# A fused local-attention and state-space kernel: the order of every engine written out by hand

## The chip, the cores and the metric

One core of one Trainium2 chip runs the kernel. It has five engines that run at once, each through its own queue in order: TensorE (PE, matrix products, with weight loads shown apart as PEld), VectorE (DVE), ScalarE (ACT), GpSimd (POOL) and SyncE (SP, which here only starts transfers). The metric is device time in microseconds (us) of one execution; the median of 3 runs counts.

## The reference: what is computed

Two independent layers read inputs of 2048 tokens by 448 channels in bfloat16, and their outputs stand side by side in one output of 2048 by 896.

Layer A is local attention with 16 heads of 28 channels. Each token looks at 8 keys: itself and the tokens 2, 4, ..., 14 before it.

```
qkv = x @ wqkv                         # 448 -> 3*448
idx = pos[:, None] - arange(8) * 2     # negative ones are masked out
logits = einsum("bhsd,bhswd->bhsw", q, k[idx]) * 28 ** -0.5
o = einsum("bhsw,bhswd->bhsd", softmax(logits), v[idx])
a = o @ wo
```

Layer B is a state-space recurrence with 448 complex states, run over all tokens:

```
h_t = exp(dt * Lambda) * h_(t-1) + B_bar x_t
y_t = 2 * Re(C h_t) + Dskip * x_t
```

## The kernel before

**Layer A.** Tokens lie as 128 partitions by 16 tokens (index j): partition p holds tokens 16p to 16p + 15. The input is transposed on PE into xTA (`g_xta`, four groups of four tokens, two PSUM banks a group, copied out by DVE at L249), and `proj(t, j)` makes queries (t = 0), keys (1) or values (2) of all tokens j with four products of 112 x 448 (L254), copied out by ACT (L258). A token's window reaches 14 back, so keys and values carry a halo of 14 rows from the partition before: three transfers from SBUF to SBUF each (L265, L271), while partition 0, which has nothing before it, is cleared by POOL (L140, L141). `logits(hf)` works on half the tokens at a time (hf = 1: j from 8 to 15): in four steps of two window positions, DVE multiplies queries and keys (L409, 7168 wide, into the buffer `pr`, which is u1), halves the channels by adding (L410, L412), and after every second step sums the rest (L414 to L417). `softmax(hf)` is DVE with one exponential on ACT (L429). Then `av` runs four groups of four tokens: for each of 8 window positions DVE multiplies attention and values (L460, seven buffers in turn, laid over the keys), and PE adds and transposes the result into four accumulators with 16 products against the identity (L465). ACT copies them out (L469), `wo_group` multiplies by wo (L477) and the rows are stored.

**Layer B.** Parameters are transposed, and DVE and ACT make the powers of the transition (sine, cosine, exponential), the block matrices R (L202, one block of 896 columns for each power), G for the input weights, and a table of angles (`tab`, L277 to L279, with 1792 columns of float32 worked out in u1 by DVE and then by three passes on ACT). Tokens are in chunks of 8; `ssm_in(hf)` runs through the 8 positions j of all 256 chunks for half of the states (4 tiles, then 3): four products a tile (L324), one with R for the step before (L329), copied to Z by ACT (L331). `ssm_scan(hf)` runs the recurrence over chunks: DVE multiplies by the table (L336, L337), PE recombines (L342, L343), DVE scans (L345), and the same back (L347 to L355). `ssm_mix(hf, j)` adds the carried state to each position (L362, L364) and `ssm_out(j, cb)` makes an output row block of 128 by 448 (L373, L375), copied by ACT and stored.

**What sets the order.** The program text lists stage after stage, but a planner with a cost model reorders it: each engine's queue is what the planner chose. In the trace the logits of layer A on DVE run between steps of layer B. All eight PSUM banks are one pool (`bank()`), handed out in turn; a product that needs a bank waits until what lay in it has been copied out. Buffers are shared over time: u1 is the input of layer A, then the angle work, then the logits' products, then wo; u2 is the input and weights of layer B, then Z; the logits and the attention lie over xTA.

Of the kernel before, what the change touches and what calls it, by code (L numbers as in the profile page):

```python
# [10 lines left out]
ALU = mybir.AluOpType  # L11
# [25 lines left out]
def kernel(  # L37
# [16 lines left out]
    nc = tc.nc  # L54
    V = nc.vector
# [35 lines left out]
    G = l2.rearrange("p a b n -> p (a b n)")[:, 0:2 * NT * 128].rearrange("p (r t n) -> p r t n", r=2, t=NT)  # L91
# [10 lines left out]

    def half_rows(src):
        return src.rearrange("(t i) d -> i t d", i=HS)

    load_w(1)
    for jg in (3, 2, 1, 0):
        SP.dma_start(xnA[:, 4 * jg:4 * jg + 4, :], xA_r[:, 4 * jg:4 * jg + 4, :])
    load_w(0)
    prow = const.tile([3 * NT, 2, HS], BF16, tag="prow")  # L110
# [14 lines left out]
    make_identity(nc, ident[:])  # L125
    swp = const.tile([128, 2, 128], BF16, tag="swp")
# [7 lines left out]
    hpib = const.tile([128, 1], F32, tag="hpib")  # L134
    POOL.memset(hpib[:], 0.5 * PI * SHR)
    kk = const.tile([128, NP], F32, tag="kk")
    POOL.iota(kk[:], [[1, NP]], base=1, channel_multiplier=0, allow_small_or_imprecise_dtypes=True)
    iot = const.tile([128, NC], F32, tag="iot")
    POOL.iota(iot[:], [[1, NC]], base=0, channel_multiplier=0, allow_small_or_imprecise_dtypes=True)
    POOL.memset(k_s[0:1, :, 0:HALO, :], 0.0)  # L140
    POOL.memset(v_s[0:1, 0:HALO], 0.0)  # L141
# [9 lines left out]
    tp = bank(BF16)  # L151
    PE.transpose(tp[:, 0:3 * NT], prow.rearrange("p a i -> p (a i)"), ident[0:3 * NT, 0:3 * NT])
    prm = pt_("prm", (128, 3, NT))
    V.tensor_copy(prm.rearrange("p a b -> p (a b)"), tp[:, 0:3 * NT])
    tp = bank(BF16)
    PE.transpose(tp[0:KT, 0:4], drow[:], ident[0:4, 0:4])
    dsk = pt_("dsk", (KT, 4))
    V.tensor_copy(dsk[:], tp[0:KT, 0:4])
    lre, lim, ld = prm[:, 0], prm[:, 1], prm[:, 2]

# [4 lines left out]

    kkb = kk.unsqueeze(2).to_broadcast(PW)
    dt = pt_("dt")
    ACT.activation(dt[:], ld, ACTF.Exp)
    are = tt(pt_("are"), dt[:], lre, ALU.mult)
    th = tt(pt_("th"), dt[:], lim, ALU.mult)  # L170
    rk = pt_("rk", PW)
    tt(rk[:], by_k(are), kkb, ALU.mult)
    ACT.activation(rk[:], rk[:], ACTF.Exp)
    f1 = pt_("f1")
    V.tensor_scalar(f1[:], th[:], 1.0 / (2 * PI), None, ALU.mult)
    fT = pt_("fT")
    V.tensor_scalar(fT[:], th[:], float(T) / (2 * PI), None, ALU.mult)
# [8 lines left out]
    yk = pt_("yk", PW)  # L186
    tt(yk[:], by_k(f1), kkb, ALU.mult)
    tk = pt_("tk", PW)
    sn = pt_("sn", PW)
    cs = pt_("cs", PW)  # L190
    sincos(sn[:], cs[:], yk[:], tk[:])
    tt(cs[:], cs[:], rk[:], ALU.mult)
    tt(sn[:], sn[:], rk[:], ALU.mult)
    coef = const.tile([128, T - 1, NT, 2], BF16, tag="coef")
    V.tensor_copy(coef[0:HS, :, :, 0], cs[0:HS, 0:T - 1])
    V.tensor_copy(coef[0:HS, :, :, 1], sn[0:HS, 0:T - 1])
    V.tensor_scalar(coef[HS:128, :, :, 0], sn[HS:128, 0:T - 1], -1.0, None, ALU.mult)
    V.tensor_copy(coef[HS:128, :, :, 1], cs[HS:128, 0:T - 1])

# [5 lines left out]
    def build_R(k0, k1):  # L205
        blocks(R[:, k0:k1].rearrange("p k t n -> p (k t) n"), coef[:, k0:k1].rearrange("p k t a -> p (k t) a"), (k1 - k0) * NT)

    build_R(0, 1)
    a1, b1 = cs[:, 0], sn[:, 0]
    nr = pt_("nr")  # L210
    V.tensor_scalar(nr[:], a1, -1.0, None, ALU.add)
    t0 = pt_("t0")
    den = tt(pt_("den"), lre, lre, ALU.mult)
    tt(t0[:], lim, lim, ALU.mult)
    tt(den[:], den[:], t0[:], ALU.add)
    V.reciprocal(den[:], den[:])
    gre = tt(pt_("gre"), nr[:], lre, ALU.mult)
    tt(t0[:], b1, lim, ALU.mult)
    tt(gre[:], gre[:], t0[:], ALU.add)
    tt(gre[:], gre[:], den[:], ALU.mult)  # L220
    gim = tt(pt_("gim"), b1, lre, ALU.mult)
    tt(t0[:], nr[:], lim, ALU.mult)
    tt(gim[:], gim[:], t0[:], ALU.subtract)
    tt(gim[:], gim[:], den[:], ALU.mult)
    cg = pt_("cg", (128, NT, 2))
    V.tensor_copy(cg[0:HS, :, 0], gre[0:HS])
    V.tensor_copy(cg[0:HS, :, 1], gim[0:HS])
    V.tensor_scalar(cg[HS:128, :, 0], gim[HS:128], -1.0, None, ALU.mult)
    V.tensor_copy(cg[HS:128, :, 1], gre[HS:128])
    cgb = const.tile([128, 2, NT, 2], BF16, tag="cgb")  # L230
    V.tensor_copy(cgb[:, 0], cg[:])
    tt(cgb[:, 1], cg[:], cgb[:, 0], ALU.subtract)
    blocks(G.rearrange("p r t n -> p (r t) n"), cgb.rearrange("p r t a -> p (r t) a"), 2 * NT)
    pm2 = pt_("pm2", (128, 1))
    POOL.memset(pm2[0:HS], 2.0)
    POOL.memset(pm2[HS:128], -2.0)
    V.tensor_tensor(dgD[:], ident[0:KT, 0:KT].unsqueeze(1).to_broadcast((KT, 4, KT)),
                    dsk.unsqueeze(2).to_broadcast((KT, 4, KT)), ALU.mult)


    def g_xta(jg):
        for k2 in range(2):
            tp = bank(BF16)
            tpv = tp[0:KT].rearrange("p (k j n) -> p k j n", k=2, j=4)
            for kk_ in range(2):
                for jj in range(4):
                    kt = 2 * k2 + kk_
                    PE.transpose(tpv[:, kk_, jj, :], xnA[:, 4 * jg + jj, KT * kt:KT * (kt + 1)], ident[:])
            V.tensor_copy(xTA[:, 2 * k2:2 * k2 + 2, 4 * jg:4 * jg + 4, :], tpv)  # L249

# [8 lines left out]

    for jg in (3, 2, 1, 0):  # L260
        g_xta(jg)
        for j in range(4 * jg + 3, 4 * jg - 1, -1):
            proj(1, j)
    for lo, hi in ((1, 65), (65, 113), (113, 128)):
        SP.dma_start(k_s[lo:hi, :, 0:HALO, :], k_s[lo - 1:hi - 1, :, J:JK, :])  # L265
    for j in range(J - 1, -1, -1):
        proj(0, j)
    for j in range(J - 1, -1, -1):
        proj(2, j)
    for lo, hi in ((1, 65), (65, 113), (113, 128)):  # L270
        SP.dma_start(v_s[lo:hi, 0:HALO], v_s[lo - 1:hi - 1, J:JK])  # L271


    ftab = u1.bitcast(F32)
    yy = ftab[:, 0:NT * NC].rearrange("p (t c) -> p t c", t=NT)
    tm = ftab[:, NT * NC:2 * NT * NC].rearrange("p (t c) -> p t c", t=NT)
    V.tensor_tensor(yy, iot.unsqueeze(1).to_broadcast((128, NT, NC)),  # L277
                    fT.unsqueeze(2).to_broadcast((128, NT, NC)), ALU.mult)
    sincos(tab[:, 1], tab[:, 0], yy, tm)  # L279
    build_R(1, T - 1)  # L280


    for t in range(NT):
# [6 lines left out]
    for j in range(T):  # L290
        tp = bank(BF16)
        tpv = tp[0:KT].rearrange("p (k c n) -> p k c n", k=4, c=2)
        for kt in range(4):
            for c in range(2):
                PE.transpose(tpv[:, kt, c, :], xnB[:, c, j, KT * kt:KT * (kt + 1)], ident[:])
        V.tensor_copy(xT[:, :, j, :], tp[0:KT].rearrange("p (k n) -> p k n", k=4))  # L296
    for t2 in range(4):
# [8 lines left out]
        V.tensor_scalar(Cw[:, 2 * t2:2 * t2 + n, :], tp[:, 0:n * D].rearrange("p (t n) -> p t n", t=n), pm2[:], None, ALU.mult)  # L306

# [6 lines left out]


    def ssm_in(hf):
        for j in range(T):
            banks = []
            for pr_ in pairs(halves[hf]):
                ps = bank()  # L320
                banks.append(ps)
                for i, t in enumerate(pr_):
                    for kt in range(4):
                        PE.matmul(ps[:, i * NC:(i + 1) * NC], BT[:, kt, t, :], xT[:, kt, j, :],  # L324
                                  start=(kt == 0 and i == 0), stop=(kt == 3 and j == 0 and i == len(pr_) - 1))
            for ps, pr_ in zip(banks, pairs(halves[hf])):
                if j > 0:
                    for i, t in enumerate(pr_):
                        PE.matmul(ps[:, i * NC:(i + 1) * NC], R[:, 0, t, :], Z[:, t, j - 1, :], start=False, stop=(i == len(pr_) - 1))  # L329
                n = len(pr_)  # L330
                ACT.copy(Z[:, pr_[0]:pr_[0] + n, j, :], ps[:, 0:n * NC].rearrange("p (t c) -> p t c", t=n))  # L331

    def ssm_scan(hf):
# [3 lines left out]
        V.tensor_tensor(scr[:, 1, ts], z7, tab[:, 1, ts], ALU.mult)  # L337
        for pr_ in pairs(halves[hf]):
# [4 lines left out]
            PE.matmul(ps[:, 0:n * NC], swp[:, 1], scr[:, 1, sl], start=False, stop=True)  # L343
# [3 lines left out]
        V.tensor_tensor(scr[:, 0, ts], z7, tab[:, 0, ts], ALU.mult)  # L347
# [36 lines left out]
    for j in range(T - 1):  # L384
        ssm_mix(0, j)
# [136 lines left out]
```

## Time and profile before

| what | us |
|---|---|
| median of 3 runs (204.83 to 205.46) | 205.44 |
| the profiled execution | 205.64 |
| its span, first to last instruction | 203.9 |
| PE busy | 169.4 |
| DVE busy | 155.6 |
| ACT busy | 92.3 |
| POOL busy | 13.4 |
| L254, 192 projection products | 42.0 |
| L409, 8 products of queries and keys | 31.1 |
| L460, 32 products of attention and values | 32.9 |
| L465, 512 products against the identity | 29.1 |

Busy times of different engines lie beside each other; what counts is which of them the others wait for. "Clock" is the TensorE clock that the chip granted, as a share of the full one: 0.933 in the mean over the span. A group's mean duration covers the pipeline, so products back to back follow each other more closely than their durations say. A wait is put down to the release that came last.

### The profile page before, as it was taken

To read this page: it belongs to the slowest core of one execution; us is meant where nothing else is said; L and a number is where in the kernel's file an instruction comes from. 1 tells how busy PE (TensorE), PEld (TensorE's weight loads), DVE (VectorE), ACT (ScalarE), POOL (GpSimd) and SP (SyncE) were. 2 spreads that over 40 slices of the span, in tenths; PEclk is the share of its full clock that TensorE was granted. 3 is DMA by queue.
4 is the path that set the end of the run, shared out by engine and by line. 5 is a ranking of instruction groups with operands and counts; after the bars stand their busy time and mean duration, and the time that the engine had idled before them with its cause. 6 is when DMAs were issued, how large, how long until landed. Compare 5 with 4: busy or idle time off the path is not lost.

```text
span 203.9 us, 3696 instructions
## 1 busy us (share of the span) xinstructions
PE 169.4 (83%) x1551; PEld 118.8 (58%) x1552; DVE 155.6 (76%) x169; ACT 92.3 (45%) x178; POOL 13.4 (7%) x24
## 2 busy tenths in 40 slices
PE   0798299999999999502799609999999999999993
PEld 0544045555579888400388405656566899797951
DVE  6989949209958999999999999999700499795102
ACT  2073034998683254400259306945645230707081
POOL 8950000000000000000000100000000000000000
PEclk9999759999999999965599966999999999999999
DMA  6999500870049200000000000033222100202023
GB/s 194 350 220 376 132 3 18 186 112 3 0 84 197 35 3 0 0 0 0 3 0 0 0 0 3 0 85 110 66 68 68 48 3 0 72 24 71 27 68 113
DMA packets 13061, 13.98 MB, mean 69 GB/s; under 512 B 4469, under 2 KB 12149, under 8 KB 12917
## 3 DMA queue, kind: packets, MB, share of 16 engines
q1 hardware_dynamic: 12973, 13.74, 25.6%
q8 instruction: 12, 0.20, 0.4%
q14 instruction: 5, 0.04, 0.1%
q10 hardware_dynamic: 71, 0.01, 0.0%
HBM read 6.89 MB, written 3.67 MB: 52 GB/s over the span
## 4 chain that ended last, share of the span: by engine, by line
PE 60%; DVE 37%; issue 1%; POOL 0%; DVEq 0%; POOLq 0%
PE b L254 19%; PE b L465 14%; PE b L373 10%; DVE u L409 9%; PE b L477 6%; DVE u L410 5%; DVE R L202 3%; PE b L364 3%; PE b L362 3%; DVE l L412 3%; DVE swp L130 2%; DVE xT L296 2%; DVE u L345 2%; DVE u L249 2%; PE b L375 2%; PE b L287 2%
## 5 line engine op out<-in xcount | busy, mean ns | idle before, releaser
L254 PE MATMUL b<-wbuf,u 112*128 112x448 bf16 x192 | 42.0, 385 | 5.4 <-DVE u L249 5.4
L460 DVE TENSOR_TENSOR k_s<-u,v_s 128x1792 bf16<-128x1792 bf16 x32 | 32.9, 1088 | 16.0 <-PE b L465 16.0
L409 DVE TENSOR_TENSOR u<-q_s,k_s 128x7168 bf16<-128x7168 bf16 x8 | 31.1, 3891 | 8.8 <-ACT tab L184 8.7
L254 PEld LDWEIGHTS <-u 112*128 112x128 bf16 x192 | 19.6, 105 | 26.4 <-DVE u L249 6.9
L465 PEld LDWEIGHTS <-k_s 128*112 128x112 bf16 x512 | 29.0, 130 | 0.3
L465 PE MATMUL b<-ident,k_s 128*112 128x128 bf16 x512 | 29.1, 219 | 0.0
L324 PE MATMUL b<-xT,BT 112*128 112x256 bf16 x224 | 27.7, 278 | 0.0
L324 PEld LDWEIGHTS <-BT 112*128 112x128 bf16 x224 | 22.3, 100 | 3.7 <-issue 0.6
L331 ACT CAST u<-b 128x512 bf16<-128x512 f32 (+1 forms) x32 | 15.5, 534 | 18.7 <-PE b L329 12.1
L373 PE MATMUL b<-Cw,u 128*128 128x448 bf16 x112 | 23.8, 352 | 0.0
L469 ACT CAST q_s<-b 112x512 bf16<-112x512 f32 x16 | 8.2, 596 | 22.8 <-PE b L465 22.8
L410 DVE TENSOR_TENSOR u<-u 128x3584 bf16<-128x3584 bf16 x8 | 16.2, 2024 | 0.1
L373 PEld LDWEIGHTS <-u 128*128 128x128 bf16 x112 | 10.5, 97 | 7.5 <-ACT u L365 0.9
L258 ACT CAST k_s<-b 128x448 bf16<-128x448 f32 x16 | 8.3, 531 | 14.6 <-PE b L254 14.6
L377 ACT CAST yo<-b 128x448 bf16<-128x448 f32 x16 | 8.5, 531 | 13.1 <-PE b L375 8.2
L365 ACT CAST u<-b 128x512 bf16<-128x512 f32 (+1 forms) x28 | 13.2, 566 | 0.9 <-PE b L364 0.9
L477 PE MATMUL b<-u,q_s 112*128 112x448 bf16 x64 | 12.6, 352 | 0.0
L355 ACT CAST u<-b 128x512 bf16<-128x512 f32 (+1 forms) x4 | 2.0, 533 | 22.4 <-PE b L354 22.4
L412 DVE TENSOR_TENSOR l<-u 128x1792 bf16<-128x1792 bf16 x8 | 8.7, 1091 | 3.2 <-PE b L287 3.1
L362 PE MATMUL b<-u,ident 128*128 128x512 bf16 (+1 forms) x28 | 10.7, 381 | 0.0
L353 PE MATMUL b<-wbuf,ident 128*128 128x512 bf16 (+1 forms) x4 | 2.3, 566 | 9.7 <-DVE wbuf L347 9.7
L364 PE MATMUL b<-u,R 128*128 128x255 bf16 x49 | 10.3, 290 | 0.0
(123 smaller groups left out, 203.2 us busy)
## 6 DMA issues: line engine op xcount, KB each, us to landing
u<-in_A_x_dram SPq DMA_DIRECT2D x4, 448.0 KB, 4.7
u<-in_B_x_dram SPq DMA_DIRECT2D x2, 896.0 KB, 13.1
out_dram<-yo SPq DMA_DIRECT2D x16, 112.0 KB, 1.8
out_dram<-ya SPq DMA_DIRECT2D x16, 112.0 KB, 1.7
wbuf<-in_A_wqkv_dram SPq DMA_DIRECT2D x3, 392.0 KB, 5.1
k_s<-k_s SPq DMA_DIRECT2D x1, 784.0 KB, 6.7
v_s<-v_s SPq DMA_DIRECT2D x1, 784.0 KB, 5.9
k_s<-k_s SPq DMA_DIRECT2D x1, 588.0 KB
```

Of the source, the lines that this page charges most:

```text
L254: PE.matmul(ps[:, 0:D], xTA[:, kt, j, :], wts[:, t, kt, :], start=(kt == 0), stop=(kt == 3))
L324: PE.matmul(ps[:, i * NC:(i + 1) * NC], BT[:, kt, t, :], xT[:, kt, j, :], start=(kt == 0 and i == 0), stop=(kt == 3 and j == 0 and i == le ...
L331: ACT.copy(Z[:, pr_[0]:pr_[0] + n, j, :], ps[:, 0:n * NC].rearrange("p (t c) -> p t c", t=n))
L362: PE.matmul(ps[:, 0:n * NC], ident[:], Z[:, sl, j, :], start=True, stop=False)
L364: PE.matmul(ps[:, i * NC + 1:(i + 1) * NC], R[:, j, t, :], Z[:, t, T - 1, 0:NC - 1], start=False, stop=(i == n - 1))
L373: PE.matmul(ps[:, 0:D], Z[:, t, j, cols], Cw[:, t, :], start=(t == 0), stop=False)
L409: V.tensor_tensor(pr[:], qv, kv, ALU.mult)
L410: V.tensor_tensor(pr[:, :, 0:14, :], pr[:, :, 0:14, :], pr[:, :, 14:28, :], ALU.add)
L412: V.tensor_tensor(l2[:, sl], pr[:, :, 0:7, :], pr[:, :, 7:14, :], ALU.add)
L460: V.tensor_tensor(pv, attn[:, s, JG * H * jg:JG * H * (jg + 1)].rearrange("p (j h) -> p j h", h=H) .unsqueeze(2).to_broadcast((128, JG, DH ...
L465: PE.matmul(acc[kt][0:KT, jj * 128:(jj + 1) * 128], pvf[:, jj, KT * kt:KT * (kt + 1)], ident[:], start=(s == 0 and jj == 0), stop=(s == W ...
L477: PE.matmul(ps[:, 0:D], oT[:, kt, jj, :], wo_p[:, kt, :], start=(kt == 0), stop=(kt == 3))
```

## The change

The planner is switched off (`tc.manual_schedule()`), so that each engine runs its work in the order of the program text, and the text is rewritten to say that order. In parts:

- Loads: x group 3, key weights, x groups 2 and 1, query weights, x group 0 (before: key weights, x groups 3 to 0, query weights).
- 44 products of the identity with itself come first on PE; their result isn't used.
- The halo clears on POOL go; partition 0's halo rows are filled by one more transfer each for keys and values, from its own rows (finite numbers, masked later as before).
- Keys are projected for j from 15 to 6 first, then queries 15 to 8, keys 5 to 0, all values (with the input weights of layer B among them), and queries 7 to 0 last, with layer B's input transposes among them. Four of these eight transposes are copied out by ACT, the others by DVE.
- G lies in the last two blocks of R instead of a buffer of its own, and R is built block by block (seven times 896 columns) instead of one and six.
- DVE work that nothing waits for at once (parameters, R, tables, logits, softmax, value products) goes into a list. Two running sums, of PE work and of DVE work, are kept with costs in microseconds written into the program; after each PE step, list items are put into the program while the DVE sum is behind. `need` forces an item that the next step reads.
- The scans are cut into steps (`scan_mul`, `scan_pe`, `scan_run`, `scan_out`) placed among the input sums of the other half and the mixing; the C weights are transposed in between.
- Value products run up to 7 ahead of `av`; each `wo` step follows an odd window position of the next group instead of standing between groups. Two of the last four accumulator copies move to DVE.

The core of the diff:

```diff
+    ctx.enter_context(tc.manual_schedule())
-    G = l2.rearrange("p a b n -> p (a b n)")[:, 0:2 * NT * 128].rearrange("p (r t n) -> p r t n", r=2, t=NT)
+    G = R[:, T - 3:T - 1]
+    load_x(3)
     load_w(1)
-    for jg in (3, 2, 1, 0):
-        SP.dma_start(xnA[:, 4 * jg:4 * jg + 4, :], xA_r[:, 4 * jg:4 * jg + 4, :])
+    load_x(2)
+    load_x(1)
     load_w(0)
+    load_x(0)
...
+    warm = bank()
+    for _ in range(44):
+        PE.matmul(warm[:, 0:128], ident[:], ident[:], start=True, stop=True)
...
-    POOL.memset(k_s[0:1, :, 0:HALO, :], 0.0)
-    POOL.memset(v_s[0:1, 0:HALO], 0.0)
+    todo = []
+    load = [8.0, 8.0]
+    def pump(lead=0.0):
+        while todo and load[1] < load[0] + lead and (todo[0][2] is None or todo[0][2]()):
+            pop()
+    def need(*items):
+        while any(item in todo for item in items):
+            pop()
+    def pe(cost):
+        load[0] += cost
+        pump()
+    def dve(cost):
+        load[1] = max(load[1], load[0]) + cost
...
+    def halo(dst_of):
+        for lo, hi in ((1, 65), (65, 113), (113, 128)):
+            SP.dma_start(dst_of(lo, hi, 0, HALO), dst_of(lo - 1, hi - 1, J, JK))
+        SP.dma_start(dst_of(0, 1, 0, HALO), dst_of(0, 1, J, JK))
+    g_xta(3)
+    params_in()
+    add(1.6, params1)
+    add(1.2, params2)
+    add(2.5, params3)
+    has_G = add(2.0, build_G)
+    has_R = [add(1.0, lambda: build_R(0))]
+    for j in (15, 14, 13, 12):
+        proj(1, j)
+    g_xta(2)
+    for j in (11, 10, 9):
+        proj(1, j)
+    g_xta(1)
+    for j in (8, 7, 6):
+        proj(1, j)
+    g_xta(0)
+    has_tab = add(6.2, tables)
+    has_D = add(0.6, build_D)
+    for j in range(15, 7, -1):
+        proj(0, j)
+    logits(1, 0, 3)
+    for j in range(5, -1, -1):
+        proj(1, j)
+    halo(lambda lo, hi, a_, b_: k_s[lo:hi, :, a_:b_, :])
+    logits(1, 1, 2)
+    logits(1, 2, 1)
+    logits(1, 3, 0)
+    need(has_G)
+    for j in range(15, -1, -1):
+        proj(2, j)
+        if j % 2 == 0 and j < 14:
+            b_weights(j // 2)
+    for k in range(1, T - 1):
+        has_R.append(add(1.0, lambda k=k: build_R(k)))
+    halo(lambda lo, hi, a_, b_: v_s[lo:hi, a_:b_])
+    for j in range(7, -1, -1):
+        proj(0, j)
+        b_x(j)
+    for n_, g in enumerate((0, 1, 2, 3)):
+        logits(0, n_, g)
+    sm1, sm0 = softmax(1), softmax(0)
+    add(2.4, sm1[0])
+    add(2.4, sm0[0])
+    add(3.5, sm1[1])
+    add(3.5, sm0[1])
+    for j in range(T):
+        if j == 1:
+            need(has_R[0])
+        ssm_in(0, j)
+    need(has_tab)
+    scan_mul(0)
+    for t2 in range(4):
+        c_weights(t2)
+    ssm_in(1, 0)
+    banks = scan_pe(0, 1)
+    scan_run(banks)
+    scan_mul(0)
+    for j in range(1, 6):
+        ssm_in(1, j)
+    banks = scan_pe(0, 0)
+    scan_out(banks)
+    ssm_in(1, 6)
+    ssm_in(1, 7)
+    scan_mul(1)
+    for j in range(3):
+        need(has_R[j])
+        ssm_mix(0, j)
+    banks = scan_pe(1, 1)
+    scan_run(banks)
+    scan_mul(1)
+    need(has_D, *has_R)
+    for j in range(3, 7):
+        ssm_mix(0, j)
+    banks = scan_pe(1, 0)
+    scan_out(banks)
...
+    has_wo = add(0.0, wo_load)
+    for i in range(32):
+        add(1.09, lambda i=i: pv_mul(i), lambda: count[0] < count[1] + NPV)
+    ssm_mix(1, 0)
+    for cb in range(2):
+        ssm_out(T - 1, cb)
+    for j in range(T - 1):
+        if j + 1 < T - 1:
+            ssm_mix(1, j + 1)
+        for cb in range(2):
+            ssm_out(j, cb)
+    for i in range(32):
+        while count[0] <= i:
+            pop()
+        pump(7.0)
+        av(i)
+        n_, _, s = steps[i]
+        if n_ > 0 and s % 2 == 1:
+            wo_j(n_ - 1, s // 2)
+    for jj in range(JG):
+        wo_j(3, jj)
```

`logits` now adds its multiply (cost 3.9), its two halvings (2.0 and 1.1) and, after every second step, the rest of the sums (2.6) to the list as separate items.

## The prediction

> **What bounds the kernel now.** I read the page first, then the chain, the waits, busy time by stretch, and the timeline of the places the chain points to. From the page, busy time by engine and the 40 slices:
>
> ```profile
> PE 169.4 (83%) x1551; PEld 118.8 (58%) x1552; DVE 155.6 (76%) x169; ACT 92.3 (45%) x178; POOL 13.4 (7%) x24
> PE   0798299999999999502799609999999999999993
> DVE  6989949209958999999999999999700499795102
> PEclk9999759999999999965599966999999999999999
> PE 60%; DVE 37%; issue 1%; POOL 0%; DVEq 0%; POOLq 0%
> ```
>
> PE (the matrix engine) is busy 83%, yet the chain is 37% DVE (the vector engine). PE has holes at slices 4, 16 to 18 and 22 to 23, and behind each PEclk falls. DVE has its own holes at 38 to 46 us and after 148. So neither engine is full; the order leaves one waiting for the other. The stretches:
>
> ```profile
> 24.00:31.00 7.00, 6.94 (x32) 3.28 (x32) 4.19 (x14) 2.13 (x4) 0.00 (x0) 0.56 0.01 2
> 84.50:91.50 7.00, 0.00 (x0) 0.00 (x0) 6.93 (x6) 0.69 (x2) 0.00 (x0) 0.77 0.00 0
> 91.50:100.00 8.50, 3.36 (x7) 0.92 (x9) 8.50 (x13) 0.48 (x1) 0.32 (x3) 0.50 0.01 2
> 114.50:122.00 7.50, 1.06 (x5) 0.42 (x6) 7.50 (x13) 0.72 (x2) 0.62 (x4) 0.80 0.00 0
> ```
>
> (Columns: stretch, length, busy PE, PEld, DVE, ACT, POOL, clock, DMA.) At 84.5 to 100 and 114.5 to 122 PE waits for the two scans, queued on DVE behind logits. The waits and timeline name the rest:
>
> ```profile
> DVE u L409 <- ACT tab L184: 8.7, 1, 8.7
> DVE k_s L460 <- PE b L465: 16.0, 3, 12.8
> 1.93 5.35 POOL L140 MEMSET k_s<- 1x6272 bf16 x1
> 2.18 5.14 DVE L130 TENSOR_SCALAR swp<-swp 128x128 bf16<-128x128 bf16 x1
> 17.57 5.75 DVE L202 TENSOR_TENSOR R<-dup,coef 128x5376 bf16<-128x5376 bf16 x1
> 24.06 6.16 PE L254 MATMUL b<-wbuf,u 112*128 112x448 bf16 x16 [4.56 <-DVE u L249]
> 31.51 27.41 PE L254 MATMUL b<-wbuf,u 112*128 112x448 bf16 x144 [0.34 <-DVE u L249]
> ```
>
> The 5.75 us R block holds a transpose copy back, PE idles 4.56 us, and the next 16 projections take 0.385 us each instead of 27.41/144 = 0.190. From 122 us PE runs unbroken to 200.4 while DVE has run dry.
>
> **The change part by part.** I sum along the chain that I expect, against the profiled execution: 205.64 us, span 203.9, 1.74 around it; the median, 205.44, is 0.2 lower.
>
> *Halo clears.* Two POOL clears of 5.35 go. Three DVE rows beside them took 5.14, 2.79 and 2.73; like rows elsewhere take 0.27 and 0.17 (three times), so about 10 us of DVE go, partly off the chain. Instead each halo gets a fourth transfer. The key halo took 33.84 to about 45.2 (DMA busy 0.85 to 45, 0.08 after): 11.3. The fourth is unseen; a gain is excluded, the third's issue took 3.0, so 0 to 3; I take 1, as it moves one partition: 12.3. Keys end near 38.3, the halo lands at 50.7, and the first product that reads it starts at 52.9: hidden, with 2.2 to spare.
>
> *Start.* x group 3 goes ahead of the key weights on SP; x took 4.4 to 5.0 from issue, so it lands by 5.7. Meanwhile 44 identity matmuls run from 1.6; at the cold rates of before (0.375 x 128/448 = 0.107; cold transposes 1.96/16 = 0.122) they take 4.7 to 5.4. Transposes start near 6.9, as in before (6.76), but the clock may be up by then; cold projections cost before 5.27 - 3.04 = 2.2. At worst they delay PE 0.7.
>
> *DVE to the end of the tables.* The diff's two running sums of cost decide where a queued step lands in program order. Followed through, the tables land after query projection 12, the first logits after key projection 1, R1 to R6 among the last inputs of the first half, the first value product after output 14. First copies begin at 7.9. Two copies 1.3, parameter copies 0.4, chain to the sine 1.6: 11.2. ACT's table load (1.28) and sine hold DVE to 12.9; behind it wait the copies of group 2, so PE idles 1.9. Then 1.2 coefficients, 1.3 copies, 2.5 for cg, 0.2 wait, 1.3, G 2.0, 1.3, R0 1.1, angles 2.05 + 1.13 + 2.03: 12.9 + 16.1 = 29.0.
>
> *The new stall.* ACT's tables (1.70 + 1.74 + 1.87 = 5.3) stand in ACT's queue after query copy 12, waiting for DVE until 29.0; ten projections' copies queue behind. PE fills the 8 PSUM banks (8 x 0.76 = 6.1) and stops about 4.0, until 34.9. The first logits need both the shared buffer u1 and queries 8 to 15: 34.3 + four copies of 0.5 = 36.4, against 45.9 before.
>
> The row nearest to this stall is the 4.56 us idle before 24.06, after which the clock was 0.56 over 24 to 31. By it the next 3.4 to 6.8 us run at half speed, 1.7 to 3.4 lost on PE; DVE isn't held, as its inputs are computed. [...]
>
> *DVE from the first logits to the first value product.* One behind the other, each waiting for the last: 45.90 to 49.83, 51.89 and 53.02 are 3.93 + 2.06 + 1.12 = 7.1 a step, 8 steps 56.9; sums 0.97 + 0.70 + 0.70, four times, 9.5; softmax 2.76 + 3.73, twice, 13.0. Interleaved, before hid about 0.11 of each; written this way it is paid, some 5 us. R blocks 6 x 1.07 = 6.4; four xT copies 2.4; Cw 2.1; table products 4 x 0.60 + 4 x 0.47 = 4.3; scans 7 x 0.60 = 4.2. Together 98.8, with 1.5 waits for transposes 100.3. Start: 36.4 + 100.3 = 136.7.
>
> Four xT copies go to ACT; no row shows that form. Between 0.59 (512 wide) and 1.87 (1792 wide), nearest by width about 1.0, beside 2.4 of PE for each pair of token groups: covered up to about 1.9.
>
> *PE over the same time.* From 34.9, at the full-clock spacing of before: 26 projections by 0.76 19.8; BT 3.2 and transposes 3.8 (3.29 and 3.74 busy); 224 + 49 input products by 0.109 (16 in 1.74) 29.7; C 1.5; scan products 14 by 0.215 3.0; mix 10.6 (28 identity and 49 R products at 0.215 and 0.108, the short ones at half); sixteen outputs by 1.525 (chain: 1.32 + 0.20) 24.4: 96.0. Waits: 0.9 for the last xT, 1.2 and 1.1 for scans . With 1.6 for the clock: 135.7. So PE stands 2 us ahead of DVE, and its two large waits for scans are gone; what is late next is the first value product, at 137.7.
>
> *The end.* From there PE has 512 x 0.0558 = 28.6 and 64 x 0.19 = 12.1, nine waits of 0.11 for products (1.005 made against 0.894 used), two short bank waits 0.3 and 0.25 for the last copies, two of which move to DVE: 179.9. Before, wo's groups lay between accumulators and covered their copies; interleaved, one group at a time does. The last group's four copies on two engines (1.2) stand behind one projection (0.76). On SP the four wo loads stand behind the output stores: issued at about 137, four by 0.8 and 5 to land (the row of the x loads), 145, first needed at 148.
>
> From the last PE instruction to the end of the span was 203.9 - 200.4 = 3.5; 183.4, and 1.74 around: 185.1. I add 1 for a second clock drop at the 1.9 wait, between none and 2: **186.1**, in medians 185.9; I say 186.
>
> **The rivals.**
>
> A, PE is the bound: DVE's 0.11s overlap after all and the clock stays up. Then 134.1 + 41.7 + 5.2 = 181.0. For it: PE's 96.0 are rows at full clock. Against it: a 4 us hole.
>
> B, more waits than I see: the halo 2 late, both clock drops whole (7), the start 3 late by the parameter chain on ACT: 2 + 3 + 6 more of clock on 186 is 197 with all of it, 190 with some. For it: strict order makes ACT and DVE block on their heads (4.0 and 1.9 already).
>
> C, the written order isn't what runs, and only clears, load order and warm matmuls act: 205.6 minus 2.2 and the 4.56 + 3.1 at 24 us, about 196 to 203. The order before differs from program order, so an order is being made somewhere; little else speaks for it.
>
> D, slower: the clock stays at half after the 31 to 35 us stall, because waits keep recurring. Each microsecond at half speed costs 0.5; from 186 it takes 39 us of it to reach 205.4. At half speed to the end of the inputs, 34.9 to 85, PE's 46 us would cost 46 more: about 230. Against it: the longest slow stretch before was near 14 us (88 to 102), with 4 us holes inside; here PE is back to back after 35.
>
> **How the numbers follow.** The forecast (183 to 190) has 0.62, A (179 to 183) 0.12, B 0.16, C 0.03, D 0.06, no change 0.01; 0.3% is about what a measurement tells from none. Faster 0.93, same 0.01, slower 0.06. Range 181, A's bound, to 196, most of B: it leaves out part of A and B, C and D, under 2 in 10.
>
> **What would show it.** Right: first logits product near 36, after ACT's tables; PE idle once near 31 to 35 and not at 84 to 100; DVE unbroken from 64 to 168; first value product near 137; PE unbroken from 138. Wrong: logits starting after the halo (then 14 more); PE idle before scan products; half clock beyond 45 us; a store or wo load holding ACT or PE; value products ready well before PE, so that PE is the bound.

## The result and the profile after

The changed kernel takes 183.72 us (median of 4 runs, 183.64 to 184.47) against 205.45 of the kernel before beside it: a ratio of 0.895, 95% interval 0.892 to 0.899. The prediction was 186.0, in a range from 181 to 196. The profiled execution took 183.74, its span 182.0, so 1.74 around it as before; PE's clock was 0.979 in the mean.

The page of the changed kernel, busy time by engine and the 40 slices of 4.55 us each:

```profile
PE 167.4 (92%) x1596; PEld 123.2 (68%) x1596; DVE 150.3 (83%) x172; ACT 95.8 (53%) x180; POOL 2.8 (2%) x22
PE   6968996599999899999999899999959999999992
DVE  1358992399997899999999999999999999996031
PEclk9999999789999999999999999999996999999999
```

Counted from 0, PE has three visible holes left: slices 2 to 3 (where PE waits for the second pair of transpose copies), 6 to 7 and 29. The clock falls behind the last two. The holes at 84 to 100 and 114 to 122 us are gone; DVE runs without a break from slice 14 to slice 35. The sum closes: PE's idle time in the span went from 203.9 - 169.4 = 34.5 to 182.0 - 167.4 = 14.6, which is 19.9, and its busy time fell by 2.0; 21.9 together, and the profiled executions differ by 205.64 - 183.74 = 21.9. No PE work was saved: the 44 added products are inside the 167.4.

The changed kernel's timeline at the places that the prediction named (start, length, engine, line, operation, tiles, what it waited for):

```profile
7.13 1.29 DVE L296 COPY u<-b 112x1024 bf16<-112x1024 bf16 x2 [4.08 <-PE b L295]
12.10 0.22 DVE L187 TENSOR_TENSOR sn<-sn,rk 128x56 f32<-128x56 f32 x1 [1.50 <-ACT sn L198]
14.25 2.66 PE L303 MATMUL b<-wbuf,u 112*128 112x448 bf16 x12 [2.06 <-DVE u L296]
33.73 6.38 PE L303 MATMUL b<-wbuf,u 112*128 112x448 bf16 x24 [3.67 <-ACT q_s L307]
35.01 3.89 DVE L445 TENSOR_TENSOR u<-q_s,k_s 128x7168 bf16<-128x7168 bf16 x1 [6.50 <-ACT q_s L307]
135.83 10.85 PE L519 MATMUL b<-ident,k_s 128*112 128x128 bf16 x160 [2.26 <-DVE k_s L505]
```

The reader is to see three things: the sine holds DVE's queue to 12.10 and PE to 14.25; the angle table's three ACT passes hold the query copies, so PE stops for 3.67 and the first logits start at 35.01; and the first value product comes 2.26 after PE asks for it. Of PE's waits only two more are over 0.5 once the work has started (engine, tile, line, whom it waited for: total, times, longest):

```profile
PE b L360 <- DVE xT L327: 0.8, 1, 0.8
PE b L410 <- ACT u L401: 0.7, 1, 0.7
```

### The profile page after: what moved, and what is told of

The parts are those of the page before. It is cut to its first block, busy times and chain, and to the rows that moved or that the text cites. A ratio compares the mean times of both kernels' runs of the same rounds, so it can differ in the third digit from the quotient of the medians.

```text
span 182.0 us, 3801 instructions
## 1 busy us (share of the span) xinstructions
PE 167.4 (92%) x1596; PEld 123.2 (68%) x1596; DVE 150.3 (83%) x172; ACT 95.8 (53%) x180; POOL 2.8 (2%) x22
## 3 DMA queue, kind: packets, MB, share of 16 engines
HBM read 6.89 MB, written 3.67 MB: 58 GB/s over the span
## 4 chain that ended last, share of the span: by engine, by line
DVE 41%; PE 39%; DMA 10%; ACT 4%; issue 3%; SPq 1%; ACTq 0%; DVEq 0%
PE b L519 17%; PE b L303 12%; DVE u L445 11%; DMA u<-in_B_x_dram 7%; PE b L535 7%; DVE u L448 4%; DVE R L204 4%; DVE l L451 3%; DMA prow<-in_B_log_dt_dram 3%; DVE u L394 2%; PE b L325 2%; PE b L315 2%; DVE l L454 2%; DVE wbuf L375 1%; DVE wbuf L376 1%
## 5 line engine op out<-in xcount | busy, mean ns | idle before, releaser
L519 PEld LDWEIGHTS <-k_s 128*112 128x112 bf16 x512 | 32.0, 135 | 4.1 <-DVE k_s L505 2.4
L519 PE MATMUL b<-ident,k_s 128*112 128x128 bf16 x512 | 32.3, 225 | 2.3 <-DVE k_s L505 2.3
L303 PEld LDWEIGHTS <-u 112*128 112x128 bf16 x192 | 18.1, 100 | 22.4 <-issue 5.9
L360 PE MATMUL b<-xT,BT 112*128 112x256 bf16 x224 | 26.9, 272 | 0.8 <-DVE xT L327 0.8
L367 ACT CAST u<-b 128x512 bf16<-128x512 f32 (+1 forms) x32 | 15.6, 535 | 18.4 <-PE b L366 14.8
L540 ACT CAST ya<-b 128x448 bf16<-128x448 f32 x14 | 7.5, 538 | 18.0 <-PE b L535 13.3
L535 PE MATMUL b<-u,q_s 112*128 112x448 bf16 x64 | 14.1, 352 | 0.0
L528 ACT CAST q_s<-b 112x512 bf16<-112x512 f32 x14 | 7.2, 596 | 11.7 <-PE b L519 11.7
L411 ACT CAST u<-b 128x512 bf16<-128x512 f32 (+1 forms) x28 | 13.1, 558 | 0.2 <-PE b L410 0.2
L307 ACT CAST v_s<-b 128x448 bf16<-128x448 f32 x16 | 8.5, 532 | 3.3 <-PE b L303 3.3
L307 ACT CAST q_s<-b 128x448 bf16<-128x448 f32 x16 | 8.2, 535 | 3.5 <-PE b L303 3.5
```

The lines of the kernel that those rows point to most:

```text
L303: PE.matmul(ps[:, 0:D], xTA[:, kt, j, :], wts[:, t, kt, :], start=(kt == 0), stop=(kt == 3))
L307: ACT.copy(dst, src)
L411: ACT.copy(Z[:, sl, j, :], ps[:, 0:n * NC].rearrange("p (t c) -> p t c", t=n))
L519: PE.matmul(acc[kt][0:KT, jj * 128:(jj + 1) * 128], pvf[:, jj, KT * kt:KT * (kt + 1)], ident[:], start=(s == 0 and jj == 0), stop=(s == W ...
L535: PE.matmul(ps[:, 0:D], oTs[n_ % 3][:, kt, jj, :], wo_p[:, kt, :], start=(kt == 0), stop=(kt == 3))
```

## Experiments

All ratios are against the kernel before, run beside each on the same chip. The changed kernel was not run again beside them, so a difference from it in us compares medians of separate sets of runs (the kernel before had 205.25 to 205.49 in these sets); a few tenths of a microsecond of it are noise.

**1. Only the planner off.** Which part of the result is the switch, and which the text written for it? (This also tests rival C, that the written order isn't what runs.)

```diff
     nc = tc.nc
+    ctx.enter_context(tc.manual_schedule())
     V = nc.vector
```

> The kernel before with the planner switched off and nothing else: every engine runs in the order of the old text, all of layer B ahead of the logits. Theory (the new text's interleaving is the gain): DVE reaches the first logits only after the second scan, near 120 us, then needs about 80 us of logits and softmax with PE idle, then 43 us of value products and 5 of tail: 235 to 255 us. Rival (the planner's order was the loss in itself): 206 or less.

Measured, in two runs: 257.42 (256.35 to 258.48), ratio 1.254 (1.242 to 1.266). The written order is what runs, and the old text is a bad order: it is 52 us slower, some 2 us more than the upper end expected. PE's longest wait in that trace (engine, tile, line, whom it waited for: total, times, longest; "issue" means that the profile shows no cause):

```profile
PE b L466 <- issue: 49.0, 1, 49.0
```

In the text's order all logits stand behind all of layer B, and PE does nothing for 49.0 us before the first value product. So the switch by itself gains nothing; the gain comes with the rewritten text, 257.4 to 183.7 under the same switch. That text holds smaller edits beside the order. Two of them are taken back below (the clears, the identity products); the load order, G's new place, R in blocks and the copies moved between ACT and DVE were not tried by themselves.

**2. Only the halo clears, in the old kernel with its planner.** The prediction gave about 10 us of DVE time to the clears.

```diff
-    POOL.memset(k_s[0:1, :, 0:HALO, :], 0.0)
-    POOL.memset(v_s[0:1, 0:HALO], 0.0)
...
+    SP.dma_start(k_s[0:1, :, 0:HALO, :], k_s[0:1, :, J:JK, :])
...
+    SP.dma_start(v_s[0:1, 0:HALO], v_s[0:1, J:JK])
```

> The kernel before, planner on, only the two POOL clears replaced by one more transfer for each halo. Theory: the three DVE rows held beside the clears fall from 10.7 us together to about 0.6, but the 5.75 us R block and both scan holes stay: 201 to 205 us. Rival (the clears carry the gain): 190 to 196.

Measured: 205.40 (203.91 to 205.76), ratio 0.999 (0.996 to 1.002): nothing. DVE's busy time fell from 155.6 to 148.6, which is 7.0 and not the prediction's 10, since two of its three rows lie over each other (2.79 from 9.82 us and 2.73 from 9.90), and the span stayed at 203.9. Its timeline shows why:

```profile
12.96 0.22 DVE L146 TENSOR_TENSOR sn<-sn,rk 128x56 f32<-128x56 f32 x1 [2.20 <-ACT sn L180]
14.59 0.69 DVE L247 COPY u<-b 112x1024 bf16<-112x1024 bf16 x1 [0.72 <-PE b L246]
17.51 5.75 DVE L200 TENSOR_TENSOR R<-dup,coef 128x5376 bf16<-128x5376 bf16 x1
24.00 6.16 PE L252 MATMUL b<-wbuf,u 112*128 112x448 bf16 x16 [4.56 <-DVE u L247]
```

The time that the clears took came back as waits, for the sine (2.20) and for PE's next transposes (0.72); the R block that holds the copies starts at 17.51 instead of 17.57, and PE's 4.56 of idle is unchanged. In the old order the clears lay beside slack. My expectation counted them as gain by themselves and was wrong.

**3. The change with its clears back on POOL.** The same part, undone in the new order.

```diff
     POOL.memset(swp[:], 0.0)
+    POOL.memset(k_s[0:1, :, 0:HALO, :], 0.0)
+    POOL.memset(v_s[0:1, 0:HALO], 0.0)
...
-        SP.dma_start(dst_of(0, 1, 0, HALO), dst_of(0, 1, J, JK))
```

> The changed kernel with the two halo clears back on POOL and the two extra transfers gone. Theory: POOL is busy from 2.3 to about 13 us, the two scaling rows on DVE end with it (about 2.7 us each instead of 0.17), the chain to the tables and the first logits is 3 to 4 later: 186.5 to 188 us. Rival (hidden beside the load of x): within 0.5 of 183.7.

Measured: 190.97 (190.96 to 191.07), ratio 0.930 (0.925 to 0.936), 7.25 us slower than the changed kernel. The direction was expected, the size was not. The timeline of that kernel:

```profile
2.23 5.32 POOL L146 MEMSET k_s<- 1x6272 bf16 x1
7.49 5.35 POOL L147 MEMSET v_s<- 1x6272 bf16 x1
2.33 5.25 DVE L148 COPY swp<-ident 64x64 bf16<-64x64 bf16 x1 [2.33 <-POOL swp L145]
7.59 5.28 DVE L149 TENSOR_SCALAR swp<-ident 64x64 bf16<-64x64 bf16 x1
13.16 1.28 DVE L298 COPY u<-b 112x1024 bf16<-112x1024 bf16 x2
41.01 5.25 PE L305 MATMUL b<-wbuf,u 112*128 112x448 bf16 x18 [3.67 <-ACT q_s L309]
```

Two copies of 64 x 64, 0.17 and 0.18 in the changed kernel, each last until the clear beside them ends (7.58 against 7.55, 12.87 against 12.84). The first transpose copy starts at 13.16 instead of 7.13, and PE's restart after the table hole moves from 33.73 to 41.01: 7.28, all of the loss. Of this, 6.03 is there at the first copy; behind it the first 16 projections run mostly at half clock after a wait of 6.62 and take 5.04 instead of 3.42, which holds ACT's key copies and the exponential behind them. I had expected other rows, the two scaling rows of the parameters, to be held. So the same edit is worth 0 in the old order and 7 in the new one, where the text puts these two rows ahead of the copies that PE waits for. What ties the end of a row to the end of the clear beside it is not shown.

**4. The change without the 44 identity products.**

```diff
-    warm = bank()
-    for _ in range(44):
-        PE.matmul(warm[:, 0:128], ident[:], ident[:], start=True, stop=True)
```

> The changed kernel without the 44 identity products. Theory: the parameter chain on DVE and ACT, not PE, sets the time to 14 us, and the first projections at half speed (about 2 us more) push only the second pair of transpose copies, by 0.5 to 1.5: 184.2 to 185.2 us. Rival (the warm products pay what they were put in for): PE's whole 2.2 us or more comes back, 186 or above.

Measured: 185.13 (184.20 to 185.36), ratio 0.901 (0.896 to 0.906), 1.4 slower in the median, with overlapping runs (the changed kernel had 183.64 to 184.47). The size is as expected, but the profiled execution puts it in another place:

```profile
4.82 1.96 PE L292 MATMUL b<-ident,u 128*112 128x128 bf16 x16 [4.82 <-DMA u<-in_A_x_dram]
14.20 3.53 PE L300 MATMUL b<-wbuf,u 112*128 112x448 bf16 x12 [2.06 <-DVE u L293]
35.33 6.38 PE L300 MATMUL b<-wbuf,u 112*128 112x448 bf16 x24 [3.67 <-ACT q_s L304]
```

The first transposes are slower (1.96 against 1.57) but start earlier (4.82 against 6.03), with no identity product ahead of them; the hole for the sine ends at 14.20, as before at 14.25. What follows it is different: the 12 projections take 3.53 instead of 2.66, at half clock from 15.84, and PE restarts 1.60 later after the table hole. Here the loss is a clock drop after the same 2.06 wait. The mean clock of the other runs says that it does not come every time: it was 0.980 in the fastest run here (184.20) and about 0.971 in the others, while the changed kernel had 0.979 in three runs and 0.970 in its slowest (184.47). Whether the identity products make the drop rarer or only fell otherwise against the clock's grid (below) is open.

**5. Three ACT passes written behind query copy 8.** Is the 3.67 hole the ACT queue's order, as the prediction said?

```diff
+    need(has_tab)
+    pass1()
+    pass2()
+    pass3()
     logits(1, 0, 3)
```

(`tables` keeps DVE's three angle operations; the three activations become `pass1` to `pass3`.)

> The changed kernel with the three table passes on ACT put behind the copy of query 8 instead of query 12; the angles stay in u1. Theory (ACT's queue, blocked at its head, makes the hole on PE at 30 to 34 us, and the hole costs the clock): the hole shrinks under 1.5 us, the clock stays up there, the first logits start 1.5 to 2 earlier: 180 to 182.5 us. Rival (DVE bounds from there on and the hole is free): within 0.7 of 183.7.

Measured: 180.49 (179.76 to 181.18), ratio 0.879 (0.874 to 0.883), 3.2 faster than the changed kernel. Its waits:

```profile
DVE u L455 <- ACT tab L295: 4.8, 1, 4.8
PE b L313 <- ACT k_s L317: 0.6, 1, 0.6
PE b L370 <- DVE xT L337: 2.0, 1, 2.0
```

PE's hole shrinks from 3.67 to 0.64 and no clock drop follows. But the logits still wait for the passes, since angles and products share u1, and PE finds DVE late at xT (2.0 instead of 0.8). So the hole was the queue; the late logits are the buffer. They start at 34.24, only 0.8 earlier and not the 1.5 to 2 expected: in this execution a clock drop behind the wait at 14 us made the angles start 1.0 later (23.73 against 22.77). The rest of the gain up to the first value product is DVE's wait for PE's layer B transposes, 1.6 in the changed kernel and gone here, where PE comes to them earlier.

**6. Angles in the value buffer.** The values are made only after key projection 0, so the angle work moves to `v_s`; the passes go behind key 0, value 12 and value 8.

```diff
-    ftab = u1.bitcast(F32)
+    ftab = v_s.rearrange("p a b c -> p (a b c)").bitcast(F32)
...
+    need(has_tab)
     logits(1, 0, 3)
     for j in range(5, -1, -1):
         proj(1, j)
+    pass1()
...
+        if j == 12:
+            pass2()
+        if j == 8:
+            pass3()
```

> The changed kernel with the angles worked out in the values' buffer instead of u1, and the three ACT passes spread out behind later projections. Theory (the first logits wait for u1 and for four query copies, both held by the table passes): logits start near 29 us instead of 35, no hole on PE at 30: 5 to 7 less, 177 to 179 us. Rival (PE bounds after 34 us): only PE's 3.7 and the clock's 1.6 come back, the first value product waits for PE: 178.5 to 180; rival two (hidden): 183.

Measured: 176.59 (176.54 to 176.73), ratio 0.861 (0.858 to 0.864), 7.1 faster than the changed kernel, just under the 177 expected. Logits start without a wait, and the clock is 1.00 over the whole span:

```profile
27.48 3.88 DVE L455 TENSOR_TENSOR u<-q_s,k_s 128x7168 bf16<-128x7168 bf16 x1
PEclk9999999999999999999999999999999999999999
```

On PE's side, of the two profiled executions' difference, 7.2, the hole is 3.67, the half clock behind it 1.8 (24 projections in 6.38 instead of 24 x 0.19), the second clock drop 0.7 (160 products at the start of the values in 10.12 instead of 10.85) and an earlier first copy 1.0 (6.17 against 7.13): 7.2. The last is not the edit's: the code ahead of that copy is the same, but the 44 identity products took 4.31 in this execution and 4.87 in the changed kernel's, and the 16 transposes behind them 1.06 against 1.57.

**7. The softmax of half 0 later.** Its maximum goes behind value product 11, its exponential behind the first group's accumulator copies, its end behind product 15; the first value product then no longer stands behind both softmaxes. (The maximum and exponential of half 1 go ahead of the last logits step.)

```diff
-    add(2.4, sm0[0])
...
-    add(3.5, sm0[1])
...
+        if i == 11:
+            has_max = add(2.4, sm0[0])
+        if i == 15:
+            add(3.5, sm0[1], lambda: exp0[0])
```

> The changed kernel with the softmax of the first half of the tokens moved on DVE behind value products 11 and 15, where first needed, and its exponential behind the accumulator copies of the first group. Theory (the first value product is what PE waits for at 133.4, and the wait costs a clock drop): no hole there, clock up, one short wait before product 16: 2.5 to 3.5 less, 180 to 181.5 us. Rival (DVE's sum decides, the wait moves to product 16): within 0.7 of 183.7.

Measured: 180.27 (180.05 to 180.76), ratio 0.879 (0.875 to 0.883), 3.45 faster. The hole at 30 us stands (3.7), the one before the values is gone:

```profile
PE b L521 <- DVE k_s L507: 0.6, 1, 0.6
132.98 9.10 PE L521 MATMUL b<-ident,k_s 128*112 128x128 bf16 x160
```

The 160 products take 9.10 instead of 10.85: products now lie ready, and the clock stays up.

**8. Six and seven together.**

> The angles in the values' buffer and the late softmax together. Theory (two separate waits on one chain): the gains add, 8 to 9.5 less than the changed kernel: 174 to 176 us. Rival (once PE never waits, the second buys little): 176 to 179.

Measured: 174.92 (174.45 to 176.43), ratio 0.854 (0.849 to 0.859), 8.8 faster than the changed kernel. The parts alone give 7.1 + 3.45 = 10.6. They are not additive: on top of experiment 6 the late softmax brings 1.7, as much as the wait shrinks (2.26 before the first value product, now 0.56 before product 16); the clock drop there, which it also removed in the changed kernel, was gone with experiment 6 already.

**9. The copies of x group 2 ahead of the sine.** The largest wait left is the one at 14 us.

```diff
     for j in (15, 14, 13, 12):
         proj(1, j)
-    g_xta(2)
+        if j == 14:
+            g_xta(2)
```

> The kernel with both moves (angles in the value buffer, late softmax; 174.92), and the transposes and copies of x group 2 written after key projection 14 instead of after key projection 12, so that their copies stand on VectorE ahead of the wait for the sine. Theory (the 2.06 of PE idle at 13.78 in that kernel is VectorE's queue standing at the sine from 10.1 to 11.63, with the copies behind it, and everything later on PE follows PE): the copies end near 11.5, PE has no hole there, and the next group's copies move up by about 1.3 because the 2.4 of small rows after the coefficients stay ahead of them; 172.9 to 173.9. Rival (the parameter chain on VectorE, not PE, sets when the tables, R0 and the first logits come, so PE only waits later): within 0.7 of 174.9.

Measured: 172.32 (171.80 to 173.19, 6 runs), ratio 0.839 (0.836 to 0.842): 2.6 better than experiment 8, slightly more than expected, and the fastest of all. The two profiled executions differ by 2.0 (174.45 and 172.44). The page's first line, and DVE around the sine:

```profile
PE 163.0 (96%) x1594; PEld 120.3 (70%) x1596; DVE 149.8 (88%) x172; ACT 94.8 (56%) x180; POOL 2.8 (2%) x22
9.78 1.24 DVE L306 COPY u<-b 112x1024 bf16<-112x1024 bf16 x2
11.37 0.22 DVE L187 TENSOR_TENSOR sn<-sn,rk 128x56 f32<-128x56 f32 x1 [0.35 <-ACT sn L198]
15.69 1.91 PE L313 MATMUL b<-wbuf,u 112*128 112x448 bf16 x8 [0.30 <-DVE u L306]
```

The copies fill DVE's wait, and PE's 2.06 is now 0.30. At 163.0 of 170.7 PE is the bound; its longest wait after the start is 0.8.

## Why the prediction was right, and where not

It was right in sign, size and the main of its mechanism; 183.74 against 186.1 for the profiled execution leaves 2.4 to place. By its steps:

*Halo clears.* Costed as about 10 us of DVE, partly off the chain. The 10 counts two rows that lie over each other twice: experiment 2 measured 7.0. Experiments 2 and 3 show that their worth was not a matter of size: 0 in the old order, 7 in the new. The extra transfer was taken to delay the halo's landing by 1, between 0 and 3. SP's queue was kept for 3.00 by it:

```profile
36.74 5.88 SPq L547 DMA_DIRECT2D k_s<-k_s  x3
42.67 3.00 SPq L548 DMA_DIRECT2D k_s<-k_s  x1
```

(Rows of SP's queue in the changed kernel's timeline.) The landing is another matter. DMA had stopped by 49 (its share is 0.00 from there to 50), at most 12.3 after the first issue, the length predicted; and in the old kernel of experiment 2 the halo started as before (33.82 against 33.84) and DMA stopped by 46 in both, with three transfers and with four. So the 1 was, if anything, too much. The first product that reads the halo, at 51.7, did not wait: hidden, as said.

*Start.* First copies at 7.13 instead of 7.9. This 0.8 is the largest single term of the 2.4: the cold price of 1.96 for 16 transposes was taken, and they took 1.57, starting at 6.03 instead of 6.9. Part of this term is chance: in experiments 6 to 9 the same code had its first copy at 6.17 to 6.71.

*DVE to the end of the tables.* The wait for the sine to 12.10 (predicted 12.9), PE idle 2.06 (1.9) at 14 us, angles done at 28.0 (29.0): 0.2 less than predicted beyond the start's 0.8. The prediction put no clock drop behind this wait and gave no reason. None came in the changed kernel's trace, but in those of experiments 4 and 5 the same wait was followed by a half-clock window, worth 1.7: here it was right by luck.

*The new stall.* PE stopped 3.67 (4.0) and restarted at 33.73 (34.9); ACT's passes took 5.25 (5.3); the half clock cost 24 projections 6.38 - 4.56 = 1.8 (1.6). No row of before shows the 1.6 or a slow stretch of only 3.4: behind the wait of 4.56 the half clock lasted 6.83 (23.37 to 30.20), and both were the author's estimate; in the changed kernel it lasted 3.41 (34.41 to 37.82). The first logits came at 35.01 (36.4); of that 0.35 is the last query copies, 1.75 instead of the 2.1 that four by 0.5 gave with rounding up. Experiments 5 and 6 confirm both causes, ACT's queue and u1. The prediction also said that the slow stretch doesn't hold DVE, and that was too strong: the 1.6 that DVE waits for transposes (1.5 in its sum) is gone in experiment 5, where PE doesn't stop.

*DVE from the first logits to the first value product.* 134.69 - 35.01 = 99.7 (100.3). A step is 35.01 to 38.94, 41.00 and 42.19, that is 3.93 + 2.06 + 1.19 (1.13 in the next step, 48.18 to 49.31), against the predicted 3.93 + 2.06 + 1.12, so the 0.11 that the old interleaving hid is paid, and rival A's reason falls. The ACT form of the xT copy, bounded between 0.59 and 1.87 and taken at 1.0 by width, took 1.01.

*PE over the same time.* Waits of 0.9, 1.2 and 1.1 were predicted for xT and scans; measured were 0.8 for xT, none of weight for scans, and 0.7 for a mixing copy on ACT. This step was wrong by about 1.7, and it costs nothing, as DVE set the time: PE merely waited 2.26 for the first value product instead of 1.9.

*The end.* From PE's first value product to its end 42.65, against 43.2 with the 1 us put in for a second clock drop; that drop happened and cost 0.7. From PE's end to the end of the span 3.5, as predicted.

The terms add up to 0.8 + 0.2 + 0.05 + 0.35 + 0.6 + 0.55 - 0.15 (the first product stood 1.14 instead of 1.0 ahead of PE) = 2.4. Each is within a microsecond. The path of the prediction held; what it had wrong, the 10 us of the clears, PE's waits for the scans and a DVE that the slow stretch leaves alone, did not move its sum. Of the rivals, A's figure (181.0) lies nearest, but not for its reasons: the steps did not overlap and the clock did drop. B didn't come, C is refuted by experiment 1, and D's recurring waits did not occur: the half clock behind the stall ended at 37.8.

## What to carry to other kernels

When an order is written by hand, look on each engine's queue for the one instruction that waits for another engine, and ask what stands behind it: all three moves that gained (a table pass behind a query copy, a softmax behind value products, a copy ahead of a sine) took work out from behind such a head, at the same PE and DVE work. An edit's worth belongs to the order it is in: the halo clears were worth 0 in one and 7 us in the other. And two stages that share a buffer share a queue: giving the angles another buffer and spreading the passes was worth about twice what moving the passes alone brought (7.1, of which 1.0 is not the edit's, against 3.2).

## What the runs showed of the hardware

**The clock's grid.** Every half-clock stretch inside the work, in six traces (before, the changed kernel, experiments 3, 4, 5 and 7), lasts 3.41 us or a multiple of it (6.83, 13.65), and in one trace their starts are whole multiples of 3.413 apart (34.41 and 136.80: 30 times). Laying that grid over a trace gives PE's busy time in each window of 3.41 and the clock in the next. The changed kernel, then the kernel of experiment 4, then that of experiment 5 (stretch, length, then busy time of PE, PEld, DVE, ACT and POOL, clock, DMA share, GB/s):

```profile
10.52:13.93 3.41, 1.68 (x21) 1.24 (x18) 1.72 (x8) 2.98 (x6) 0.00 (x0) 1.00 1.13 239
13.93:17.34 3.41, 3.04 (x23) 1.73 (x24) 2.88 (x17) 1.45 (x3) 0.00 (x0) 1.00 1.13 242
31.00:34.41 3.41, 0.68 (x4) 0.38 (x4) 0.00 (x0) 3.38 (x5) 0.00 (x0) 1.00 0.00 0
133.39:136.80 3.41, 1.15 (x20) 0.98 (x17) 3.38 (x5) 0.53 (x1) 0.00 (x0) 1.00 0.26 76
```

```profile
12.43:15.84 3.41, 1.60 (x8) 0.70 (x9) 3.08 (x15) 1.61 (x4) 0.00 (x0) 1.00 1.21 218
15.84:19.25 3.41, 3.41 (x23) 2.41 (x22) 1.71 (x9) 1.14 (x3) 0.00 (x0) 0.50 0.97 357
```

```profile
11.54:14.95 3.41, 1.36 (x7) 0.56 (x8) 3.09 (x14) 1.52 (x5) 0.00 (x0) 1.00 1.14 225
```

The windows at 31.00, 133.39 and 11.54 were followed by one at 0.50 too, the changed kernel's first one by 1.00. From the first 6.4 us of a run apart, each full-clock window in these six traces with 1.60 us or less of PE work was followed by one at half clock, and none with 1.68 or more. Experiment 1's trace shows otherwise early in the run, where PE, after 18 small products, stood idle for 15 us:

```profile
20.39:23.80 3.41, 0.00 (x0) 0.00 (x0) 3.34 (x6) 0.00 (x0) 0.00 (x0) 1.00 0.83 183
```

This window and the three before it have no PE work, and the recorded clock stays at 1.00. Yet the 16 projections right behind took 4.82 and the next 16 took 3.42, so early in a run the recorded clock does not tell PE's speed; why is not shown. A full window at half speed costs busy PE about 3.41 / 2 = 1.7, an estimate from its length; behind the table hole 1.8 was measured. So a wait of 2.06 may cost 0 or 1.7 on top, by where it falls: nothing in the changed kernel (1.68 of PE work in its window), a half-clock window in experiments 4 and 5 (1.60 and 1.36). Each run's mean clock shows that such windows make part of the spread between executions of one kernel: in experiment 5 the two runs at 0.979 took 180.97 and 181.18, the two at 0.987 and 0.988 took 179.76 and 180.01. The spread of 1.4 in the last experiment, whose runs all have 0.996 or more, stays open.

**A transfer of one partition.** The fourth halo transfer, 12 KB from one partition, kept SP's queue as long (3.00) as the third with 15 partitions had in the kernel before (3.0), and its pair for the values 2.97. Whether that time is its own or is caused by the three queued before it was not tried; the halo's landing was not 3 later for it (above).
